# Ten more unread 512-column products on TensorE in the first attention of a fused attention and MLP kernel

## Chip, cores and metric

The kernel runs on one core of one Trainium2 chip. The metric is device time in microseconds (us). One core has five engines with queues of their own: TensorE (matrix products and transposes; PE in the profile, with its weight loads as PEld), VectorE (DVE), ScalarE (ACT), GpSimd (POOL) and SyncE (SP), and 16 DMA engines.

## What is computed

q, k and v have 8 batches, 8 heads, 576 positions and 64 elements a head. The first four heads attend to the last 32 positions (local), the other four to earlier positions of the same residue modulo 32 (strided). The result, as 4608 rows of 512, goes through an MLP with the Mish activation.

```python
mask_local   = (rel >= 0) & (rel < 32)
mask_strided = (rel >= 0) & (pos[None, :] % 32 == pos[:, None] % 32)
attn = softmax(where(mask, q @ k.T / 8, -1e9)) @ v        # per batch and head
x = attn.transpose(0, 2, 1, 3).reshape(4608, 512)
h = x @ w_in                                              # 512 -> 2048
out = (h * tanh(softplus(h))) @ w_out                     # 2048 -> 512
```

## The kernel before, in words

**Order.** The kernel writes its order out by hand (`tc.manual_schedule()`, L636): each engine executes its instructions in the order in which the code issues them, and the framework adds semaphore waits where tiles depend on each other. The attention of batch 0 stands alone at the start (L677 to L721). After it, a loop over nine blocks of 512 rows (L745) issues two MLP products a block, L575 (x times w_in, into `psh`) and L599 (g times w_out, into `pso`), and weaves the attention of later batches between them.

**PSUM.** Products write to PSUM. There are three accumulators, `acc(0)` to `acc(2)`, of one buffer each (L90), and one small tile `tile_t` with two buffers in turn (L94). A new tile in an accumulator waits until all who wrote or read the old one are done.

**First attention.** Small loads are issued first: k of two strided heads over SyncE and ScalarE, all others over GpSimd (strided k, q and v, then the local k and q as `lq`, then local v, then w_in in five chunks, then the next batch and w_out). On TensorE the steps are:

- 88 products of 64 columns into `acc(2)` (L678), on zeroes from the tile `kTs[1]`, which nobody reads.
- `t_step` (L230) transposes strided k, then q, 8 transposes for each pair of heads (`hp`). VectorE copies the result of the first pair out of PSUM, ScalarE that of the second.
- `a.bias` (L292) writes the mask as a large negative number into an accumulator by a product with the identity, and `a.qk` (L302) adds the scores on top of it; then ScalarE takes exp into `Ps` (strided) or `Pl` (local). The strided scores are in three parts, s0 to s2, as are the local ones, l0 to l2.
- `a.pv2` (L388) multiplies the weights by v for two of the eight strided indices (or two of the six local windows) into an accumulator; VectorE then takes a reciprocal (L396) and multiplies (L397) into `x_s` or `x_l`. In batch 0 each strided product is two instructions, of 64 columns (L366) and of 1 (L371).
- `t_step_loc0` (L248) transposes the local k (`kl0`) and q (`ql0`) with 24 transposes for each of them, and ScalarE copies them out.
- `a.xt` (L402) transposes `x_s` and `x_l` into `xT`, the input of the MLP.

**Fills.** `fill` (L544) issues n products of 512 columns whose result is never read; `fill_acc` (L551) does so into an accumulator, `fill(tile_t(..))` into the small tile. Their operands are the zeroed part of `kTs[1]`. Before the change there are seven of 512 columns: three ahead of the q transposes (L682), one ahead of the bias of s2 (L686), two ahead of the first `pv2` (L690) and one ahead of the bias of l2 (L709).

Of the kernel before, what the change touches and what calls it, by code (L numbers as in the profile page):

```python
# [40 lines left out]
def kernel(ctx, tc, q, k, v, moe_w_in, moe_w_out, out):  # L41
# [48 lines left out]
    def acc(i, name):  # L90

        return ps_a.tile([128, 2, 512], F32, tag=f"acc{i}", name=name)

    def tile_t(name):  # L94
        return ps_t.tile([128, 512], F32, tag="pt", name=name)


    def sT(x, b):

        return x[(b + 1) % 2 if b else 0]  # L100
# [40 lines left out]
    def rows_v_loc01(b, hp, eng):  # L141
        x = vl[b % 2][:, :, 2 * hp:2 * hp + 2, 0:D]
        cast(eng, x[0:32, 1:NW], x[96:128, 0:NW - 1])
# [33 lines left out]
    def cast(eng, out_, in_):  # L177
        if eng is nc.scalar:
            nc.scalar.copy(out_, in_)  # L179
        else:  # L180
            eng.tensor_copy(out_, in_)  # L181
# [48 lines left out]
    def t_step(b, which, hp, eng=None):  # L230

        eng = eng or nc.vector
        tr = tile_t("tr")[:].bitcast(BF16)
        src = (qs if which == "q" else ks)[b % 2]
        for u in range(8):
            h, jj = 2 * hp + u // 4, u % 4
            nc.tensor.transpose(
                tr[:, PN * u:PN * u + PN],
                src[0:PN, h, 128 * jj:128 * jj + 128],
                ident[0:PN, 0:PN],  # L240
            )
        dst = sT(qTs if which == "q" else kTs, b)[:, 8 * SU * hp:8 * SU * hp + 8 * SU]
        cast(
            eng, dst.rearrange("c (u n) -> c u n", u=8)[:, :, 0:PN],
            tr[:, 0:S].rearrange("c (u n) -> c u n", u=8),
        )

    def t_step_loc0(src, dst, hp, eng):  # L248

        tr = tile_t("tr")[:].bitcast(BF16)  # L250
        for j in range(CL):
            for e in range(2):
                nc.tensor.transpose(  # L253
                    tr[64 * e:64 * e + 64, PL * j:PL * j + PL], src[0:PL, 2 * hp + e, j, :],
                    ident[0:PL, 0:PL],
                )
        cast(
            eng, dst.rearrange("c (p j) -> c p j", j=CL),
            tr[:, 0:S].rearrange("c (j p) -> c p j", j=CL),
        )  # L260
# [283 lines left out]
    def fill(t, n, w=512):  # L544

        for _ in range(n):
            nc.tensor.matmul(
                t[:, 0:w], lhsT=kTs[1][:, 512:640], rhs=kTs[1][:, 0:w], start=True, stop=True
            )

    def fill_acc(i, n, w=512):  # L551
        fill(acc(i, "fill")[:, 0, :], n, w)
# [83 lines left out]
    with tc.manual_schedule():  # L636
        Po, Dv, Sc = nc.gpsimd, nc.vector, nc.scalar
# [38 lines left out]

        a = Attn(0)  # L677
        fill_acc(2, 88, 64)  # L678
        for hp in range(2):
            t_step(0, "k", hp, Sc if hp else Dv)  # L680
        a.bias("s", 0, 0)
        fill_acc(2, 3)  # L682
        for hp in range(2):
# [3 lines left out]
        a.bias("s", 2, 2)  # L687
        for i in range(3):
            a.qk([("s", i)], i)
        fill(tile_t("fill"), 2)  # L690
        a.pv2("s", 0, 0)
        t_step_loc0(kl0, kTl[:, 0, 32:32 + S], 0, Sc)
        t_step_loc0(kl0, kTl[:, 1, 32:32 + S], 1, Sc)
        a.pv2("s", 2, 1)
        t_step_loc0(ql0, qTl[:, 0, :], 0, Sc)
        t_step_loc0(ql0, qTl[:, 1, :], 1, Sc)
        a.bias("l", 0, 1)
        a.pv2("s", 4, 2)
        a.qk([("l", 0)], 1)
        a.pv2("s", 6, 0)  # L700
        a.bias("l", 1, 2)
        a.qk([("l", 1)], 2)
        for hp in range(2):
            rows_v_loc01(0, hp, Dv)
        load_v_loc_h(1)
        load_w_out(3, 4)
        a.xt("s", 0, Dv)
        a.xt("s", 1)
        fill_acc(0, 1)  # L709
        a.bias("l", 2, 0)  # L710
        a.qk([("l", 2)], 0)
        Sc.preload_act_table(AF.Mish)
# [119 lines left out]
```

## Time and profile before

| | us |
|---|---|
| median of 4 runs | 307.38 |
| the runs | 306.56, 307.35, 307.42, 312.17 |
| the profiled execution, whole | 306.78 |
| its span, first to last instruction | 305.0 |

The span is what the profile's rows count from; 1.8 us of the profiled execution lie around it. A few more rows matter, with start and length in us. On ScalarE, the three exps of the strided scores:

```profile
10.00 2.20 ACT L338 ACTIVATE Ps<-ps 72x864 bf16<-72x864 f32 x3 [0.71 <-PE ps L324]
12.11 1.18 ACT L179 COPY kTl<-tr 128x576 bf16<-128x576 bf16 x2
13.68 1.18 ACT L179 COPY qTl<-tr 128x576 bf16<-128x576 bf16 x2 [0.39 <-PE tr L253]
```

On TensorE, the transposes of the local q and the start of the MLP:

```profile
13.19 0.70 PE L253 MATMUL tr<-consts_sb,lq 96*64 96x96 bf16 x24 [0.34 <-DMA lq<-in_q_dram]
...
19.69 1.02 PE L575 MATMUL psh<-xT,w_in 128*128 128x512 bf16 x4 [0.47 <-DVE rden L396]
```

A bracket at the end of a row gives the engine's idle time ahead of it and what ended it. A row's length runs from the first start to the last end, and the end of a product is modelled with the time it takes to drain, so a gap on TensorE is best read from one start to the next.

### The profile page before, as it was taken

The numbers are of one execution on the slowest core, as the hardware profiler recorded it, in microseconds if no ns is written. First come the engines' busy times: TensorE is split into PE (matmuls) and PEld (weight loads), VectorE is DVE, ScalarE is ACT, GpSimd is POOL, SyncE is SP. The second block draws the span as 40 slices with busy tenths as digits, with TensorE's granted clock in tenths as the row PEclk, the third lists the DMA queues.
The fourth block names the chain that finished last, engine by engine and source line by source line (L and its number), as shares of the span: only waits on it lengthen the run. The fifth ranks groups of instructions, "written<-read, shape, count | busy, mean of one in ns | idle before, by whom it ended". The sixth has DMA issues, their size and how long they took to land.

```text
span 305.0 us, 6113 instructions
## 1 busy us (share of the span) xinstructions
PE 298.2 (98%) x2547; PEld 159.8 (52%) x2547; DVE 155.3 (51%) x375; ACT 181.4 (59%) x193; POOL 105.0 (34%) x119
## 2 busy tenths in 40 slices
PE   8999999999999999999999999999999999999995
PEld 7665556444554455444579554445444444444444
DVE  4382266202840086489877888788878850000000
ACT  2676634776456754757965786678668756116501
POOL 8652439930372034402970297028500000000000
PEclk9999999999999999999999999999999999999999
DMA  7999999999999999999989996996520120011011
GB/s 131 166 198 186 203 179 139 153 107 263 178 214 121 199 165 190 159 177 197 187 171 184 188 167 145 176 194 110 129 88 0 56 83 0 2 69 69 0 71 69
DMA packets 97551, 41.83 MB, mean 137 GB/s; under 512 B 79604, under 2 KB 91460, under 8 KB 97524
## 3 DMA queue, kind: packets, MB, share of 16 engines
q1 hardware_dynamic: 71708, 28.84, 55.4%
q0 software_dynamic: 25504, 12.31, 35.2%
q8 instruction: 20, 0.33, 0.5%
q10 hardware_dynamic: 312, 0.28, 0.3%
q14 instruction: 7, 0.06, 0.1%
HBM read 36.82 MB, written 9.44 MB: 152 GB/s over the span
## 4 chain that ended last, share of the span: by engine, by line
PE 90%; DVE 3%; DMA 3%; POOL 1%; issue 1%; ACT 1%; ACTq 0%; POOLq 0%
PE psh L575 41%; PE pso L599 35%; PE pso L626 5%; PE po L366 4%; PE ps L324 3%; DMA lq<-in_q_dram 3%; DVE x_l L383 1%; PE trx L410 1%; DVE x_s L383 1%; PE tr L253 1%; DVE rden L382 1%; PE trx L420 1%; PE ps L297 0%; ACT Ps L338 0%; POOL qs L110 0%
## 5 line engine op out<-in xcount | busy, mean ns | idle before, releaser
L575 PE MATMUL psh<-xT,w_in 128*128 128x512 bf16 (+3 forms) x648 | 130.6, 355 | 0.7 <-DVE rden L396 0.5
L599 PE MATMUL pso<-w_out,gT 128*128 128x512 bf16 x512 | 121.7, 379 | 0.0
L581 ACT ACTIVATE gT<-psh 128x1024 bf16<-128x1024 f32 x72 | 72.4, 1023 | 46.1 <-PE psh L575 46.1
L575 PEld LDWEIGHTS <-w_in 128*128 128x128 bf16 x648 | 60.7, 98 | 55.3 <-issue 1.1
L599 PEld LDWEIGHTS <-gT 128*128 128x128 bf16 x512 | 45.5, 98 | 46.1
L445 DVE STREAM_TRANSPOSE xs_t<-x_s 32x512 bf16<-32x512 bf16 x48 | 33.7, 702 | 0.9
L606 ACT COPY osb<-pso 128x1024 f32<-128x1024 f32 x16 | 17.6, 1101 | 24.8 <-PE pso L599 14.4
L382 DVE RECIPROCAL rden<-po 72x4 f32<-72x4 f32 (+1 forms) x98 | 17.3, 177 | 28.6 <-PE po L366 28.5
L181 POOL CAST kl<-kl 96x768 bf16<-96x768 f32 x10 | 8.7, 897 | 62.4 <-DMA kl<-in_k_dram 55.0
L436 DVE STREAM_TRANSPOSE xT<-x_l 32x384 bf16<-32x384 bf16 x48 | 27.3, 569 | 0.7
L181 DVE COPY osb<-pso 128x512 f32<-128x512 f32 (+1 forms) x2 | 1.1, 558 | 51.3 <-PE pso L626 51.3
L346 DVE TENSOR_TENSOR Ps<-Ps,consts_sb 72x864 bf16<-72x864 bf16 (+3 forms) x12 | 6.6, 552 | 40.0 <-ACT Ps L338 40.0
L383 DVE TENSOR_TENSOR x_s<-po,rden 72x256 bf16<-72x256 f32 x56 | 23.5, 421 | 1.9
L338 ACT ACTIVATE Ps<-ps 72x864 bf16<-72x864 f32 (+3 forms) x21 | 17.4, 861 | 11.1 <-PE ps L324 11.1
L366 PEld LDWEIGHTS <-Ps 72*128 72x128 bf16 x256 | 15.7, 97 | 11.7 <-DVE Ps L346 0.8
L452 ACT COPY xT<-xs_t 128x576 bf16<-128x576 bf16 x8 | 21.4, 2938 | 0.0
L338 ACT ACTIVATE Pl<-ps 128x960 bf16<-128x960 f32 (+1 forms) x20 | 17.3, 875 | 2.8 <-PE ps L324 2.8
L383 DVE TENSOR_TENSOR x_l<-po,rden 96x256 bf16<-96x256 f32 x42 | 17.7, 421 | 1.4
L366 PE MATMUL po<-vs,Ps 72*128 72x65 bf16 (+1 forms) x256 | 18.3, 194 | 0.1
L179 ACT COPY xT<-trx 128x576 bf16<-128x576 bf16 x15 | 9.6, 638 | 12.9 <-PE trx L420 9.1
L181 POOL CAST vl<-vl 128x768 bf16<-128x768 f32 (+2 forms) x20 | 15.5, 777 | 4.7 <-DMA vl<-in_v_dram 3.3
L346 POOL TENSOR_TENSOR Ps<-Ps,consts_sb 72x1008 bf16<-72x1008 bf16 (+1 forms) x9 | 14.5, 1642 | 1.2 <-ACT Ps L338 1.1
(93 smaller groups left out, 241.9 us busy)
## 6 DMA issues: line engine op xcount, KB each, us to landing
out_dram<-osb SPq DMA_DIRECT2D x16, 512.0 KB, 4.1
kl<-in_k_dram SPq DMA_DIRECT2D x5, 576.0 KB, 7.0
ql<-in_q_dram SPq DMA_DIRECT2D x5, 576.0 KB, 11.9
vs<-in_v_dram SPq DMA_DIRECT2D x5, 576.0 KB
vl<-in_v_dram SPq DMA_DIRECT2D x5, 576.0 KB, 9.9
w_out<-in_moe_w_out_dram POOLq DMA_DIRECT2D x4, 512.0 KB, 15.4
ks<-in_k_dram POOLq DMA_DIRECT2D x7, 288.0 KB, 10.4
qs<-in_q_dram POOLq DMA_DIRECT2D x7, 288.0 KB, 11.0
```

The costliest lines, as they stand in the source:

```text
L181: eng.tensor_copy(out_, in_)
L338: nc.scalar.activation(pt[0:n, :, 0:nw], t[0:n, :, o0:o0 + nw], AF.Exp, scale=scale)
L346: meng.tensor_tensor(out=pm, in0=pm, in1=mk[0:n, :].unsqueeze(1).unsqueeze(1).to_broadcast([n, 2, nu, w]), op=ALU.mult,)
L366: nc.tensor.matmul(po[:, h, 0:rhs.shape[-1]], lhsT=pt[0:n, c0:c0 + 128], rhs=rhs, start=True, stop=True,)
L382: nc.vector.reciprocal(rden[0:m, :], po[0:m, :, D])
L383: nc.vector.tensor_tensor(out=dst.rearrange("p (h d) -> p h d", h=4), in0=po[0:m, :, 0:D], in1=rden[0:m, :].unsqueeze(2).to_broadcast([m, ...
L436: nc.vector.transpose(dst[32 * q:32 * q + 32, :, :, m:m + 32], src[m:m + 32, :, :, q, :])
L445: nc.vector.transpose(xs_t[32 * q:32 * q + 32, :, :, m:m + 32], src[m:m + 32, :, :, q, :])
L452: nc.scalar.copy(xT[:, 2 + c, t0:t0 + S].rearrange("p (n j) -> p j n", j=CS), xs_t[:, :, c, 0:PN])
L575: nc.tensor.matmul(ps[:, u, o:o + n], lhsT=w_in[:, cc, fc * 128:(fc + 1) * 128], rhs=xT[:, cc, a:a + n], start=(cc == 2 and o == 0), stop= ...
L581: nc.scalar.activation(gT[:, 2 * g:2 * g + 2, :], ps[:], AF.Mish)
L599: nc.tensor.matmul(p[:, ot % 2, :], lhsT=gT[:, fc, 128 * ot:128 * ot + 128], rhs=w_out[:, fc, :], start=(fc == 0), stop=(fc == 15),)
```

## The change

Products of 512 columns that nobody reads are put in at six more places or added to those there, all in the first attention. The change's heading speaks of nine; the diff has ten.

```diff
         a = Attn(0)
         fill_acc(2, 88, 64)
-        for hp in range(2):
-            t_step(0, "k", hp, Sc if hp else Dv)
+        t_step(0, "k", 0, Dv)
+        fill_acc(2, 2)
+        t_step(0, "k", 1, Sc)
         a.bias("s", 0, 0)
...
-        fill(tile_t("fill"), 2)
+        fill(tile_t("fill"), 3)
         a.pv2("s", 0, 0)
+        fill(tile_t("fill"), 1)
         t_step_loc0(kl0, kTl[:, 0, 32:32 + S], 0, Sc)
         t_step_loc0(kl0, kTl[:, 1, 32:32 + S], 1, Sc)
         a.pv2("s", 2, 1)
+        fill_acc(0, 2)
         t_step_loc0(ql0, qTl[:, 0, :], 0, Sc)
         t_step_loc0(ql0, qTl[:, 1, :], 1, Sc)
         a.bias("l", 0, 1)
         a.pv2("s", 4, 2)
+        fill_acc(0, 1)
         a.qk([("l", 0)], 1)
         a.pv2("s", 6, 0)
         a.bias("l", 1, 2)
         a.qk([("l", 1)], 2)
+        fill(tile_t("fill"), 2)
         for hp in range(2):
             rows_v_loc01(0, hp, Dv)
...
         a.xt("s", 1)
-        fill_acc(0, 1)
+        fill_acc(0, 2)
         a.bias("l", 2, 0)
```

The two transposing steps of k, a loop before, are written out so that two products fit between them. Nothing else in the kernel differs.

## The prediction

> **What bounds the kernel now.** I read the page first, then the chain of work that ended last, then TensorE's own timeline over the first 20 us.
>
> ```profile
> span 305.0 us, 6113 instructions
> ...
> PE 298.2 (98%) x2547; PEld 159.8 (52%) x2547; DVE 155.3 (51%) x375; ACT 181.4 (59%) x193; POOL 105.0 (34%) x119
> ...
> PEclk9999999999999999999999999999999999999999
> ```
>
> TensorE is busy 98% of the span, and the chain is 90% TensorE. From 19.69 us on, where the first product of the MLP (L575) starts, the later part of the chain is products in a row with short detours through VectorE and ScalarE that themselves hang on products. The loads of w_in land long before their use (the trace has the second of the five chunks done at 19.62 and first read at 20.80, and the last one done at 28.23 and first read at about 30.6). The longest later wait, 0.4 us at 44.54, ends with VectorE's x_s, not with a DMA (its ql landed at 40.04). So a delay of the L575 start at 19.69 us goes through to the end. The question is by how much that start moves.
>
> ```profile
> 5.24 7.91 DMA lq<-in_q_dram
> 13.15 0.04 issue
> 13.19 0.70 PE tr L253 x24
> ...
> 15.15 0.70 DVE x_s L397
> 15.85 0.05 issue
> 15.90 0.58 PE ps L297 x2
> 16.48 0.32 PE ps L324 x10
> 16.79 0.63 PE trx L420 x16
> 17.42 0.23 PE fill L547
> ...
> 18.85 0.69 DVE x_l L397
> ```
>
> This is the chain in order of time (start, length, what). The local q lands at 13.15, and what TensorE does before it is off the path as long as it is done by then. After 13.15 the path is TensorE, one VectorE normalization, and from 15.90 TensorE without a break up to the last po products.
>
> ```profile
> 1.27 4.87 PE L547 MATMUL fill<-kTs 128*128 128x64 bf16 x88 [1.27 <-DVE kTs L651]
> 5.95 1.01 PE L237 MATMUL tr<-consts_sb,ks 72*128 72x72 bf16 x16
> ...
> 7.16 0.81 PE L547 MATMUL fill<-kTs 128*128 128x512 bf16 x3
> 7.93 0.68 PE L237 MATMUL tr<-consts_sb,qs 72*128 72x72 bf16 x16
> ...
> 10.21 0.60 PE L547 MATMUL fill<-kTs 128*128 128x512 bf16 x2
> 10.94 0.20 PE L366 MATMUL po<-vs,Ps 72*128 72x64 bf16 x1
> ...
> 17.26 0.38 PE L547 MATMUL fill<-kTs 128*128 128x512 bf16 x1
> 17.70 0.32 PE L297 MATMUL ps<-consts_sb 128*128 128x192 bf16 x2
> ```
>
> TensorE's timeline (start, length, line, tiles). A length includes some 0.17 us of modelled latency, so I work with distances between starts. Two things are to be seen. The 16 transposes of k take 1.01 us and the 16 of q 0.68: less the 0.20 of the last one, 15 steps at 54 against 32 ns. The page's clock row shows no throttle, but the array ran at half speed up to about 6.66 us: 60 ns a step for some 12 steps, 33 after that. And after one fill at 17.26 the bias into the same PSUM tile starts only 0.44 later, not 0.22: it waits for the fill to be complete.
>
> **The change, part by part.** The listing of the changed kernel has 20 TensorE rows more, ten products and their ten weight loads: ten, not nine. [...] The price of one is 0.215 us (four L575 products of the same shape start within 0.86). Ten are 2.15 us; what waits cover is taken off, in order. A delay means: later than in the trace of before.
>
> *Two between the k transposes (start 6.43).* At half speed up to 6.66, the first takes 0.33 and the second 0.215; the eight transposes behind them then run at 33 instead of some 45 ns, 0.10 back. TensorE is 0.44 late. The three fills at 7.16 ended at 7.81; the q transposes then waited until 7.93 for qs to land, 0.12 of cover. Delay 0.32. Scores, and with them ScalarE's first exp (10.00, ScalarE idle before it), are 0.32 later.
>
> *A third fill ahead of the first pv2.* The two at 10.21 are done at 10.66, and pv2 starts at 10.94, when the exp is done. The wait of 0.28 covers the 0.215. Delay still 0.32, now set by the exp.
>
> *One behind the first pv2.* pv2's last product leaves at about 11.40; the kl0 transposes start at 11.62 because lq lands at 11.58 and because a change from full to 64-column products costs 0.095 (seen at every such change in this stretch). With the delay: 11.72 + 0.215 + 0.095 = 12.03. Delay 0.40. kTl copies and exps on ScalarE move by 0.32, which makes no new wait.
>
> *Two behind the second pv2.* That ends at 12.71 + 0.40 = 13.11, the two at 13.54, and the ql0 transposes start at 13.64 instead of 13.19: the DMA wait of 0.51 covers most of this part and of what came before. Delay 0.45. The first fill waits for VectorE to have read accumulator 0 (12.50 + 0.32 = 12.82), already past, so it holds up nothing queued behind it. bias l0 then waits for x_s on VectorE (13.82 + 0.40), so 0.40 remains.
>
> *One behind the third pv2.* It delays q times k of l0 by 0.57 to 0.64, but the bias of l1 at 15.90 waits for VectorE's x_s of the third pv2, which was issued ahead of the fill. TensorE stands at 16.21, the bias starts at 16.30. Covered on TensorE; delay 0.40. The fourth pv2's normalization comes 0.57 late, at 17.35, before the transposes that read it.
>
> *Two ahead of the x_s transposes, and a second at the end.* Here there is no cover. From 15.90 to 18.6 the chain above is TensorE alone. The two start at 16.63 + 0.40 + 0.10 and add 0.43 + 0.01; the transposes were 0.1 late for that same change of shape already. The second of the last group adds 0.215; the completion wait of 0.44 was there before. Delay 0.40 + 0.44 + 0.215 = 1.06.
>
> *Behind that.* The last exp, pv2 of l and VectorE's x_l hang on these products and shift by the same 1.06; ScalarE's table load at 18.76 becomes 19.82 to 21.1 and is still done before the xT copy at 22.06. L575 starts at 20.75. The same accumulators go round, tile_t ends on the same one of its two buffers, and no DMA is issued by TensorE. DMA engines get no work and only a little more time.
>
> Sum: 305.0 + 1.06 = 306.06 span, or 306.78 + 1.06 = 307.84 for the profiled execution, which lies 0.60 below the median of 307.38. On the median: **308.44**, 0.34% more.
>
> **What the notes say of the clock, weighed.** The row first: from 6.66 to 19.7 no TensorE wait is longer than 0.7 us, and the spacing stays at full speed throughout, with the transposes at 32 ns. The Trainium skill, "TensorE: Matmul & The Clock Gate", Part 1 (The HAM clock gate), says that the clock is raised after a busy window of some 3.4 us that runs free of the kernel, and lowered after an idle one. By the rule, more products in short waits hold a clock that might go down; by the row there is nothing to hold, so I give that gain 0. The free window does bear on the sum: the trace shows the rise 5.4 us after the first product, and other runs may have it elsewhere. If it comes before 5.95, the k transposes end 0.3 us earlier, TensorE waits for qs, and the first two fills are hidden: 1.06 - 0.32 = 0.74. If it comes late, qs is no cover: 1.06 + 0.12 = 1.18. Other runs' phases aren't in this trace; I keep 0.74 to 1.2 as the bounds and take this trace's 1.06.
>
> **The rivals.** About 0.3% (0.92 us) is what a measurement of this kernel can tell from no change, so 306.46 and 308.30 are the lines.
>
> *Most is covered (within 0.3%).* Early clock as above, and one or two of the last three products hidden: if the x_s transposes are really held by VectorE (x_s ends at 16.78, they start at 16.73), up to 0.1 goes. That gives 0.4 to 0.85, about 308.0. For it: the waits add up to 1.3 us in this stretch. Against: the last three products stand on the chain. Also in this case: a wait downstream eats part of it; I found none that ends with something independent of TensorE.
>
> *The products hold the clock (faster).* One of the four runs of before took 312.17, 4.8 over the median. If that, and in smaller measure the ordinary runs, come from a return to half speed between 10 and 14 us, where TensorE has mostly small products and waits, the five fills added there would keep the window busy. To end below 306.46 it has to save 1.06 + 0.92, about 2 us: some 4 us at half speed in most runs of before. It then gives 307.38 + 1.06 - 2.5 = 305.9. Against it: the profiled execution shows no return and is only 0.6 below the median, and the fastest run only 0.8, so an ordinary run can't have lost 2 us that way. It would clear the slow run, not the ordinary ones.
>
> *It does not do what it says.* Were fewer products issued or moved elsewhere, the time would stay at 307.4; the listing shows all ten in their places.
>
> **How the numbers follow.** Likeliest, the sum: slower by 0.92 to 1.8 (late clock, or completion waits at the new places of 0.2 each that I have taken as covered), 308.3 to 309.2, chance 0.60. Mostly covered, 307.2 to 308.3: 0.30. Clock held, below 306.46: 0.10. The prediction is 308.4. The range 307.1 to 309.5 leaves out the clock case (0.10), a few hundredths at its foot and about 0.05 above for a new wait.
>
> **What would show it.** In the changed profile: k's second eight transposes at about 6.98; the q transposes at 8.25 with no DMA wait; ql0's transposes at 13.5 to 13.7 with no DMA wait, where 13.19 had 0.34; the first L575 at 20.7 to 20.8; from there the same distances. The clock would show in the two rows of L237: as many ns a step as before. I am wrong if L575 starts near 19.7 (covered), if the delay at 19.7 is gone by 60 us (a wait eats it), or if the spacing of the small products in other runs of before was at half speed.

## The result, and the profile after

| | before | changed |
|---|---|---|
| median, us | 307.35 (63 runs) | 307.94 (44 runs) |
| profiled execution, us | 306.78 | 307.81 |
| its span, us | 305.0 | 306.0 |
| first L575, us | 19.69 | 20.71 |

The ratio of the times is 1.0025, with a 95% interval of 1.0013 to 1.0037: slower by 0.77 us, 0.40 to 1.14. That is a loss clear of noise. Its middle is smaller than the forecast 1.06 us, which the interval still holds. The median lies inside the 0.3% that I had set as the line, and so in the case "most is covered" (0.30), not in the one called likeliest (308.3 to 309.2, 0.60). The comparison leaves out 12 of the 63 runs of before, which took over 310.9 us, and none of the 44 of the changed kernel (highest 309.79), so that the means over all runs are about equal (308.24 and 308.11) though the medians aren't.

The page of the changed kernel, its span, busy times and clock row:

```profile
span 306.0 us, 6133 instructions
...
PE 299.4 (98%) x2557; PEld 159.4 (52%) x2557; DVE 156.0 (51%) x375; ACT 181.6 (59%) x193; POOL 103.7 (34%) x119
...
PEclk9999999999999999999999999999999999999999
```

Ten products more, and 1.0 us more of span. From the first L575 to the first product of the last block's second half (L626) the two traces agree: 268.19 us in each (19.69 to 287.88 before, 20.71 to 288.90 after). So all of the difference arises ahead of the first L575. The chain in order of time (start, length, what):

```profile
4.57 7.40 DMA lq<-in_k_dram
11.97 0.04 issue
12.02 0.70 PE tr L253 x24
...
13.24 0.45 PE fill L547 x2
13.69 0.63 PE tr L253 x24
...
17.17 0.54 PE fill L547 x2
17.71 0.52 PE trx L420 x16
18.23 0.45 PE fill L547 x2
18.68 0.04 issue
18.72 0.33 PE ps L297 x2
...
19.88 0.69 DVE x_l L397
```

It starts from the landing of the local **k** at 11.97, not of the local q as before, and added products stand in it at 13.24, 17.17 and 18.23 (there one of the two). TensorE's timeline shows how far each step moved:

```profile
1.27 4.29 PE L547 MATMUL fill<-kTs 128*128 128x64 bf16 x88 [1.27 <-DVE kTs L651]
5.39 0.42 PE L237 MATMUL tr<-consts_sb,ks 72*128 72x72 bf16 x8
5.65 0.60 PE L547 MATMUL fill<-kTs 128*128 128x512 bf16 x2
...
7.96 0.68 PE L237 MATMUL tr<-consts_sb,qs 72*128 72x72 bf16 x16 [0.29 <-DMA qs<-in_q_dram]
...
10.97 0.20 PE L366 MATMUL po<-vs,Ps 72*128 72x64 bf16 x1
...
12.02 0.70 PE L253 MATMUL tr<-consts_sb,lq 96*64 96x96 bf16 x24 [0.21 <-DMA lq<-in_k_dram]
12.65 0.20 PE L366 MATMUL po<-vs,Ps 72*128 72x64 bf16 x1
...
20.71 1.02 PE L575 MATMUL psh<-xT,w_in 128*128 128x512 bf16 x4 [0.47 <-DVE rden L396]
```

The clock rose at 4.72 us here (6.66 before), so the 88 warm-up products are over 0.56 us earlier, the k transposes take 0.42 us for eight, and the two products between them are hidden: the q transposes wait 0.29 us for qs and start 0.03 us later than before. The second `pv2` starts at 12.65 (before: 12.26), and the L575 8.06 us after it (before: 7.43). So 0.39 us came ahead of the second `pv2`, and 0.63 us behind it.

### The profile page after: what moved, and what is told of

Read it like the earlier page. It is cut to its first block, busy times and chain, and to the rows that moved or that the text cites. A ratio compares the mean times of both kernels' runs of the same rounds, so it can differ in the third digit from the quotient of the medians.

```text
span 306.0 us, 6133 instructions
## 1 busy us (share of the span) xinstructions
PE 299.4 (98%) x2557; PEld 159.4 (52%) x2557; DVE 156.0 (51%) x375; ACT 181.6 (59%) x193; POOL 103.7 (34%) x119
## 4 chain that ended last, share of the span: by engine, by line
PE 91%; DVE 3%; DMA 2%; POOL 1%; issue 1%; ACT 1%; ACTq 0%; POOLq 0%
PE psh L575 41%; PE pso L599 34%; PE po L366 5%; PE pso L626 5%; PE ps L324 3%; DMA lq<-in_k_dram 2%; DVE x_l L383 1%; PE tr L253 1%; PE trx L410 1%; DVE x_s L383 1%; DVE rden L382 1%; PE fill L547 1%; PE trx L420 1%; PE ps L297 0%; ACT Ps L338 0%
## 5 line engine op out<-in xcount | busy, mean ns | idle before, releaser
L575 PE MATMUL psh<-xT,w_in 128*128 128x512 bf16 (+3 forms) x648 | 130.6, 355 | 0.7 <-DVE rden L396 0.5
L575 PEld LDWEIGHTS <-w_in 128*128 128x128 bf16 x648 | 60.8, 98 | 55.3 <-issue 1.1
```

The lines of the kernel that those rows point to most:

```text
L575: nc.tensor.matmul(ps[:, u, o:o + n], lhsT=w_in[:, cc, fc * 128:(fc + 1) * 128], rhs=xT[:, cc, a:a + n], start=(cc == 2 and o == 0), stop= ...
```

## The experiments

Theory: a product costs what no wait covers, and the waits end with landings and with VectorE's normalizations. Rivals: each product costs its 0.215 us wherever it stands; the waits cover all; the products hold the clock. I read each trace from two points, since the loads land differently in every execution: the landing of the local k, and the second `pv2`. Some product records are missing in these traces; the points used are there.

| kernel | local k landed | second pv2 | first L575 | L575 less pv2 | median us | ratio to before (95%) |
|---|---|---|---|---|---|---|
| before | 11.58 | 12.26 | 19.69 | 7.43 | | |
| changed | 11.97 | 12.65 | 20.71 | 8.06 | 307.94 | 1.0025 (1.0013 to 1.0037) |
| k2_only | 11.60 | 12.72 | 20.15 | 7.43 | 307.19 | 0.9994 (0.9977 to 1.0011) |
| last3_only | 11.33 | 12.01 | 20.07 | 8.06 | 307.62 | 1.0009 (0.9995 to 1.0022) |
| first7_only | 13.43 | 14.10 | 21.61 | 7.51 | 307.42 | 1.0004 (0.9988 to 1.0020) |
| no_end_fill | 11.85 | 12.53 | 19.52 | 6.99 | 306.82 | 0.9976 (0.9946 to 1.0007) |
| no_fill | 12.30 | 13.45 | 22.79 | 9.34 | 310.86 | 1.0110 (1.0087 to 1.0133) |
| tile_end | 12.70 | 13.38 | 22.14 | 8.76 | 309.07 | 1.0058 (1.0034 to 1.0081) |
| covered_only | 12.80 | 13.48 | 20.56 | 7.08 | 307.52 | 0.9999 (0.9973 to 1.0025) |
| changed_again | 11.55 | 12.22 | 20.28 | 8.06 | 308.29 | 1.0026 (1.0006 to 1.0046) |
| end_acc1 | 11.68 | 12.83 | 20.68 | 7.85 | 308.03 | 1.0025 (1.0011 to 1.0039) |
| five_covered | 11.25 | 12.46 | 19.54 | 7.08 | 307.11 | 0.9999 (0.9975 to 1.0024) |

The medians come from four occasions, so the ratios are compared and not the medians. In eight of the twelve rows the second `pv2` follows the landing of the local k by 0.67 to 0.68 us, and that landing alone moves by 2.2 us (11.25 to 13.43). A whole-kernel time can't separate parts of 0.1 to 0.3 us here; the last column but two can.

**The pair between the k transposes, alone** (k2_only, against the kernel before).

```diff
-        for hp in range(2):
-            t_step(0, "k", hp, Sc if hp else Dv)
+        t_step(0, "k", 0, Dv)
+        fill_acc(2, 2)
+        t_step(0, "k", 1, Sc)
```

> The kernel before with only the two products between the k transposes added. Path theory (a product costs what no wait covers up to the landing of the local q at about 13.2 us): these 0.43 us stand ahead of the waits for qs (0.12 us with this rise of the clock, more with an early one) and for the local q (0.51 us, 0.39 after the change of shape), so nothing is left: first L575 at 19.7 us, ratio 1.000, at most +0.1 us. Even-price theory (each product costs its 0.215 us): first L575 at 20.1 us, +0.43 us, ratio 1.0014.

The time didn't rise (0.9994), and from the second `pv2` on the trace is that of before, 7.43 us. But the first L575 came at 20.15 and not at 19.7: in this trace the clock rose only at 7.28, and TensorE shows the other side:

```profile
5.95 0.67 PE L237 MATMUL tr<-consts_sb,ks 72*128 72x72 bf16 x8
6.43 0.62 PE L547 MATMUL fill<-kTs 128*128 128x512 bf16 x1
7.27 0.43 PE L237 MATMUL tr<-consts_sb,ks 72*128 72x72 bf16 x8 [0.22 <-issue]
7.54 0.53 PE L297 MATMUL ps<-consts_sb 72*128 72x432 bf16 x2
7.90 0.81 PE L547 MATMUL fill<-kTs 128*128 128x512 bf16 x3
8.55 0.62 PE L237 MATMUL tr<-consts_sb,qs 72*128 72x72 bf16 x14
```

The pair ran at half speed and takes 0.84 us, from 6.43 to 7.27 (one of its two records is missing). The q transposes start at 8.55, though qs landed at 8.08, and the second `pv2` comes 1.12 us after the local k instead of 0.68. So with a late rise the pair is on the path, here for up to 0.44 us; with an early one it is free. Neither "free" nor "even price" holds: it depends on the phase.

**The last three, alone** (last3_only, against the kernel before).

```diff
         a.qk([("l", 1)], 2)
+        fill(tile_t("fill"), 2)
...
-        fill_acc(0, 1)
+        fill_acc(0, 2)
         a.bias("l", 2, 0)
```

> The kernel before with only the last three products added (two ahead of the x_s transposes, one more ahead of the bias of l2). Path theory: nothing covers them, +0.66 us, first L575 at 20.3 to 20.4 us, ratio 1.0021. Even-price theory: the same 0.65 us, so this run only tells both from the theory that waits on VectorE's x_s or on exp cover part of them, which gives +0.2 us or less, ratio 1.0007. If the first seven are free when all stand together, the whole change would be 0.66 and not 1.0.

From the second `pv2` to the L575 it takes 8.06 us, 0.63 more than before, and exactly as much as the changed kernel. The ratio, 1.0009 (0.9995 to 1.0022), holds 0.63 us (1.0020) only near its upper end. The trace decides: these three are on the path.

**The first seven, without the last three** (first7_only; its diff is that of the change without the lines above).

> The changed kernel without its last three added products, so the first seven added. Path theory: they share one cover, the wait for the local q, and together overrun it: first L575 at 20.0 to 20.1 us, +0.40 us, ratio 1.0013; the products themselves are 1.51 us. Even-price theory: +1.5 us, L575 at 21.2 us, ratio 1.0049. Full-cover theory: L575 at 19.7 us, ratio 1.000.

1.0004: far from the even price of 1.5 us, and 0.40 us (1.0013) and nothing are both inside the interval. The local k landed at 13.43 in this trace, and the second `pv2` followed it by 0.67 us, so in this trace the first four are covered, as they must be with a landing this late. Behind the second `pv2` 0.08 us remain. The fourth `pv2` comes so late that its normalization, which ends at 18.79, holds up the last of the x_s transposes: their row is 0.79 us long and not 0.69 as before, and the product behind them starts 0.63 us after them instead of 0.53.

```profile
18.55 0.79 PE L420 MATMUL trx<-consts_sb,x_s 72*128 72x72 bf16 x16
19.18 0.38 PE L547 MATMUL fill<-kTs 128*128 128x512 bf16 x1
```

**The old one at the end taken out of the kernel before** (no_end_fill).

```diff
         a.xt("s", 1)
-        fill_acc(0, 1)
         a.bias("l", 2, 0)
```

> The kernel before without its last 512-column product of the first attention (ahead of the bias of l2), none added. Path theory with the completion wait: the bias starts when the transposes are done instead of 0.44 us later, first L575 at 19.25 us, -0.44 us, ratio 0.9986. Even-price theory: -0.215 us, L575 at 19.47 us. Clock theory (these products keep the array at full speed): part of the stretch from 17 us on runs at half speed, and the time rises by up to 1 us or more.

The timeline from the x_s transposes on:

```profile
17.00 0.69 PE L420 MATMUL trx<-consts_sb,x_s 72*128 72x72 bf16 x16
17.52 0.33 PE L297 MATMUL ps<-consts_sb 128*128 128x192 bf16 x2
...
19.52 1.02 PE L575 MATMUL psh<-xT,w_in 128*128 128x512 bf16 x3
```

6.99 against 7.43 us: 0.44, the price of the completion wait and not of the product. The bias starts as soon as the transposes are through (17.00 to 17.52) where before it started 0.97 us after their start. The time points the same way (0.9976), but its interval reaches over 1.

**No 512-column products at all** (no_fill: the seven of before taken out, none added).

> The kernel before without any of its seven 512-column products of the first attention, only the 88 of 64 columns stay. Path theory alone: the six earlier ones were covered, the last cost 0.44 us, so -0.44 us like the kernel without the last alone, ratio 0.998. Clock theory: without them the array goes back to half speed in the first attention; the profile then shows a granted clock below 1 for some 7 to 10 us (0.983 or less over the span) behind about 10 us, the L575 products there run at 0.43 us instead of 0.215, and the time rises by 4 us or more, ratio 1.013 or over.

TensorE's busy time and granted clock in five stretches of this kernel's trace (the full-speed time from the rise of the clock at 6.35, then the half-speed time in quarters):

```profile
6.35:9.76 3.41, 2.46 (x54) 1.00 1.20 177
9.76:13.18 3.42, 2.28 (x63) 0.50 1.82 169
13.18:16.59 3.41, 3.41 (x65) 0.50 1.75 167
16.59:20.01 3.42, 3.42 (x57) 0.50 1.25 205
20.01:23.42 3.41, 3.14 (x40) 0.50 1.24 206
```

The columns are the stretch, its length, TensorE busy (instructions), granted clock, DMA share and GB/s. The array went back to half speed at 9.76 and stayed there until 23.42, 13.66 us, and the kernel took 1.1% more. All six runs of this kernel show a lowered mean clock (0.972 to 0.983). So the products of before do hold the clock; path theory alone failed by 1.3%, and the clock theory had put the loss a little high (1.3% or more, for 7 to 10 us at half speed). What brought it down was no long idle time: in the stretch ahead of 9.76 TensorE was busy 72%, and its longest wait was this one:

```profile
8.13 0.68 PE L237 MATMUL tr<-consts_sb,qs 72*128 72x72 bf16 x16 [0.94 <-DMA qs<-in_q_dram]
```

**The last two into the small tile** (tile_end, against the changed kernel).

```diff
         a.xt("s", 1)
-        fill_acc(0, 2)
+        fill(tile_t("fill"), 2)
         a.bias("l", 2, 0)
```

> The changed kernel with its last two products written to the small PSUM tile instead of accumulator 0, so that the bias of l2 does not wait for their completion. Path theory with the completion wait: -0.22 us against the changed kernel, from the second pv2 to the first L575 7.84 us instead of 8.06 us, ratio to the kernel before 1.0018. Even-price theory: no difference to the changed kernel, 8.06 us.

8.76 us, not 7.84. TensorE's timeline:

```profile
18.27 0.68 PE L420 MATMUL trx<-consts_sb,x_s 72*128 72x72 bf16 x16
19.72 0.59 PE L547 MATMUL fill<-kTs 128*128 128x512 bf16 x2 [0.77 <-DVE xT L181]
20.15 0.33 PE L297 MATMUL ps<-consts_sb 128*128 128x192 bf16 x2
```

The completion wait is gone (0.43 us from the first fill to the bias, the two products alone), but the small tile has two buffers, both just filled by the x_s transposes, and the fill waits 0.77 us for VectorE to copy the first of them into xT. This expectation overlooked the buffer's reader.

**The last two into accumulator 1** (end_acc1: `fill_acc(1, 2)` in their place), against the changed kernel: the same question put again.

> The changed kernel with its last two products written to accumulator 1, which l0's exp has long read and which is next written 0.45 us later by the pv2 of l, so that neither VectorE's xT copy (the wait of the small tile) nor a product's completion stands ahead of the bias of l2. Path theory with the completion wait: from the second pv2 to the first L575 7.84 us instead of 8.06 us, and 0.22 us less than the changed kernel, ratio to the kernel before 1.0018. Even-price theory: 8.06 us, ratio 1.0025.

TensorE's timeline:

```profile
18.24 0.60 PE L547 MATMUL fill<-kTs 128*128 128x512 bf16 x2
18.68 0.33 PE L297 MATMUL ps<-consts_sb 128*128 128x192 bf16 x2
```

From the first of the two products to the bias it is 0.44 us, the two products alone; in the changed kernel it was 0.66 (18.06 to 18.72). With it come 7.85 us behind the second `pv2`, as the completion wait has it: 0.21 us less than the changed kernel. (The second `pv2` stands 1.15 us behind the local k here: with the clock's rise at 7.03 the pair was on the path again.) In the whole time (1.0025) this doesn't show above the spread.

**Without the last places** (covered_only: first7_only without the old one at the end; five_covered: that without the pair between the k transposes).

> The changed kernel with its first seven added products and none in the last two places, so that the old one ahead of the bias of l2 goes too. Path theory: from the second pv2 to the first L575 7.43 + 0.08 - 0.44 = 7.07 us, and the time 0.7 to 1.0 us below the changed kernel and 0 to 0.4 us below the kernel before, ratio 0.9987 to 1.0. If the last products hold the clock, its granted clock falls below 1 in the first attention.

> The changed kernel without the two products between the k transposes and without any in the last two places, the old one ahead of the bias of l2 gone too: five added, one taken out. Path theory: 7.07 us from the second pv2 to the first L575 as in the kernel with the pair, second pv2 0.68 us behind the landing of the local k whatever the phase of the clock, 0.36 us below the kernel before, ratio 0.9988. If the pair between the k transposes is free whenever the local k lands late, no difference to the kernel with it (ratio 0.9999) can be told. If the pair is what holds the clock, the granted clock falls below 1 in the first attention.

Both take the expected 7.08 us behind the second `pv2`, and both come out at 0.9999: 0.27% under the changed kernel's 1.0026 taken beside the first of them, but no gain on the kernel before is shown. In the trace of five_covered the local k landed early, at 11.25, and the product behind the first `pv2` took its place as what the kl0 transposes wait for (11.53 to 11.83): the second `pv2` is 1.21 us behind the landing and not 0.68, so that part of my expectation was wrong. Some 0.2 us of it are the product; for the rest TensorE was still at work on the strided heads, behind the landing of qs at 7.93. No version here beats both kernels by more than the noise.

**The changed kernel again** (changed_again).

> The changed kernel once more, beside the three others. Path theory: from the second pv2 to the first L575 8.06 us as in its first trace, ratio to the kernel before 1.001 to 1.004; the place of the second pv2 itself moves with the landing of the local k and q by some tenths from run to run. If the added 1.0 us of the first trace were all due to the products, the second pv2 would start at 12.6 to 12.7 us again whenever the local k lands at 11.6 us.

1.0026 and 8.06 us, as at first; the second `pv2` started at 12.22, with the local k at 11.55. So the 0.39 us of the first trace ahead of the second `pv2` weren't the products.

## Why the prediction was right, and where it was not

*What bounds it.* Right that the start of the L575 goes through to the end. Wrong that everything ahead of 13.15 is off the path: the local k at 11.58 leads as well, over the kl0 transposes, the second `pv2` and VectorE's x_s to the bias of l0, which starts 1.61 to 1.62 us behind the second `pv2` in the traces of before, of the changed kernel and of nine of the ten others (1.83 in no_fill, at half speed). In the trace of before both chains arrived within some 0.05 us of each other at 13.88 (the x_s of the second `pv2` ended on VectorE at 13.82):

```profile
11.62 0.70 PE L253 MATMUL tr<-consts_sb,lq 96*64 96x96 bf16 x24
12.26 0.20 PE L366 MATMUL po<-vs,Ps 72*128 72x64 bf16 x1
...
13.88 0.58 PE L297 MATMUL ps<-consts_sb 128*128 128x480 bf16 x2
```

*The pair (0.32 us).* The term that was mis-sized. It took the phase of one trace for all. With the rise at 4.72 it was 0 and with the rise at 7.28 up to 0.44, as the two bounds of the prediction (early and late clock) had it. So the q transposes started at 7.96 behind a DMA wait, where the prediction's sign was 8.25 without one. Its mean over phases and landings is not settled: the interval of k2_only allows at most 0.34 us.

*The third ahead of the first pv2.* Covered as said: from the q transposes to `pv2` 3.01 us in both traces.

*The one behind it (0.08) and the two behind the second pv2 (0.05).* Small in the changed traces, as said; with the local k as early as in five_covered the first of them costs about its full length. What covers the two is VectorE's normalization as much as the local q: in the changed trace the ql0 transposes start at 13.62 without a DMA wait, and the bias of l0 still 1.61 us behind the second `pv2`.

*The one behind the third pv2.* Covered: from the bias of l0 to that of l1 2.02 us before and after.

*The last three (0.66 us).* Measured 0.63 in the trace that adds them alone. The two traces of the whole change have the same 0.63 behind the second `pv2`, so there the three products ahead of them added nothing.

*The sum.* The changed trace has 1.02 us against 1.06, and that agreement is half luck: 0.63 us are the last three, as worked out, while the other 0.39 us are a later landing of the local k, where the sum had put the pair. The time has 0.77 us (0.40 to 1.14). This fits the last three alone and the early-clock bound of 0.74, but doesn't tell them from the sum. So direction and mechanism held; "most is covered" has the better size for the first seven, not for the last three.

*The rivals.* That the products hold the clock is a real mechanism (no_fill), but the seven of before do that already where the clock held, and there the added ones had nothing to save. Where it did not hold, they seem to be what keeps it, as the prediction said of the run of 312.17. Of 172 executions of before, k2_only, last3_only and no_end_fill with a clock on record, 26 had a mean granted clock of 0.976 to 0.984 and took 310.5 to 314.0 us. Of 137 of the changed kernel and of the five others that keep the five products added from the first `pv2` to the third (first7_only, tile_end, covered_only, end_acc1, five_covered) none was under 0.994. That is a count and not a trace: none of such an execution of before was kept, and where its clock fell is not shown. "Not what it says" fell: ten more products are in the page's count.

## What to carry to other kernels

Price a filler by the wait behind it: it is free as long as the next instruction waits for something that does not depend on TensorE, and costs its full length (0.215 us here), or the completion wait (0.44 us) if the next one writes the same PSUM tile, once it stands in a chain of products. That price is paid in every execution, while holding the clock pays only in those in which it would have fallen. Before a filler changes its PSUM tile, look who still reads that tile. And take one trace's clock phase and landing times as one draw: compare distances between fixed points of the program.

## What the runs showed of the hardware

The clock's rise came anywhere from 4.7 to 7.3 us in the eleven traces that record it, though the first product always started at 1.27, and the page shows a granted clock of 1.00 ahead of it though the array runs at half speed there (53 ns a warm-up product). The half-speed time of no_fill, 13.66 us, is four times 3.41, and the clock came down at 9.76 after just 3.41 us at full speed, behind a stretch that was 72% busy, with no wait over 0.95 us. "TensorE: Matmul & The Clock Gate" (Part 1, The HAM clock gate) in the Trainium skill gives the window of some 3.4 us, which agrees; its idle window as the cause of a fall does not fit, since the clock fell here behind a stretch that was mostly busy. How full a stretch must be isn't settled, nor whether all work counts alike (1.15 of the 2.46 busy us there were transposes): tile_end and covered_only held their clock through stretches of 73% and 74% by the records, some 78% with the product in each whose record is missing.
